# Later weight stores, a regrouped output layer and a store on two queues, in a fused attention and two-layer kernel

## The chip, the cores and the metric

The kernel runs on one core of a Trainium2 chip. The metric is the device time of one execution in microseconds (us). Three timed executions of the kernel before took 1245.21, 1245.39 and 1239.18 us, so the median is 1245.21. The trace that is read below belongs to another execution of the same kernel, which took 1240.78 us.

## The reference

All inputs are float32 (the weights arrive as 64-bit values and are narrowed on the chip). Cut to what is computed:

```python
def sm_attn(qq, kk, vv):                      # softmax(scale * qq kk^T) vv, per batch and head
    s = scale * (qq @ kk.T);  s = s - s.max(-1)
    a = exp(s);  return (a / (a.sum(-1) + 1e-9)) @ vv
p_packed = sm_attn(p, k, v)                   # 8 batches, 8 heads, 32 packed rows, 64 columns
x = sm_attn(q, p_packed, p_packed)            # 576 rows per batch and head -> x: 4608 x 512
x = max(x @ w1, x @ w2, x @ w3) @ moe_w_out   # 512 -> 768 -> 512
h = x @ w_in                                  # 512 -> 2048
g = max(h, 0) + log1p(exp(-abs(h)))           # softplus
out = g @ w_out                               # 2048 -> 512
```

## The kernel before

The first 507 us of the span hold the attention and the maxout layer, batch by batch. The change touches only what follows: the last two products, called layer 3 (`h = x @ w_in` and the softplus) and layer 4 (`g @ w_out`).

Both work on the transposed activations, in five blocks of tokens (index `c`): three blocks of 2 x 512 columns and two of 2 x 384. Both use a fast matrix scheme with seven products in place of eight (`PRODUCTS`). Each product keeps float32 accuracy by splitting each operand into a high and a low part and adding three matmuls: high by high, high by low, low by high.

A block's layer 3 has eight rounds (`j`, 42 matmuls each). Its layer 4 has 28 steps (`v`, 12 matmuls each). A step of layer 4 needs the high part `ghi` (made by ScalarE, line 126) and the low part `glo` (made by VectorE, line 128) of a slice of `g`. Both are made three steps ahead: `split_g(c, v + 3)` stands behind `layer4(c, v)`. There are three buffers each, so ScalarE can make the part of step v + 3 only once TensorE has done step v. Inside a step (lines 1125 to 1142) stand two row groups `i`, two accumulators `b` (PSUM banks) and three matmuls each. The weight tile holds high parts (`wl` = 0) and low parts (`wl` = 1).

Weights come in 16 tiles per block, eight for layer 3 and eight for layer 4. In the first block (c = 0) they are made on the way. SyncE loads raw tile s (`wu`, 896 KB from `wof` for layer 4). ScalarE and VectorE split it in two parts (`split_weights`, part 0 and part 1). The finished tile `wc` (1792 KB) stays in a ring of three for use, and is also stored to memory (`wic`, `woc`; line 1017) for the later blocks, which only load it again (`get_weights`, line 1025). The raw tiles share two buffers with the raw activations `xu` of the next block (`load_x2`, line 923), so a raw tile can be loaded only after the split of an older one has freed its buffer.

The order of the work is written out by hand: each engine gets its instructions in the order in which the program issues them (a manual schedule), and executes them in that order. In the first block `jobs[v]` lists what is issued behind step v: splits, loads, sums and splits of the next block's activations. In layer 3 the lists `aside[0]` to `aside[3]` stand between the products. SyncE issues nearly all transfers, one after another; an instruction that waits there holds back those behind it.

`done[v]` lists the results: `result` (VectorE adds and transposes) and `store` (line 1162, four transfers or more on the queues that it is given). In the last block the results of the second token half leave behind steps 19 and 27, those of the first half behind step 23.

Of the kernel before, what the change touches and what calls it, by code (L numbers as in the profile page):

```python
# [8 lines left out]
F32 = mybir.dt.float32  # L9
# [10 lines left out]
def packed_attention_maxout_softplus(  # L20
# [22 lines left out]
    nc = tc.nc  # L43
# [31 lines left out]
    FP = F2 // 2  # L75
    wi32 = dram.tile([FP, P, 4, 2, P], F32, name="wi32")
    wic = dram.tile([FP, P, 2 * 7 * 2 * P], F32, name="wic")
    wof = dram.tile([len(PRODUCTS), FP, P, 2 * P], F32, name="wof")
    woc = dram.tile([FP, P, 2 * 7 * 2 * P], F32, name="woc")
# [41 lines left out]
    def split(src, hi, lo, engine=nc.vector):  # L121
        for _ in split_steps(src, hi, lo, engine):
            pass
# [717 lines left out]
    for n in range(1, B):  # L841
        for slot in range(F1 + KC):
# [22 lines left out]
            if n + 1 == B:  # L865

                if slot == 0:
# [12 lines left out]
                    pairs, wus, xus, x2 = {}, {}, {}, {}  # L880
# [24 lines left out]
                    def pair_tile(s):  # L905
                        t = ring[s % 3].tile([P, 2, 7, 2, P], F32R, tag="ring", name="wc")
                        pairs[s] = t
                        return t
# [100 lines left out]
    def split_weights(s, part):  # L1009
        if part == 0:  # L1010
            pair_tile(s)
        a, b = ((0, 4), (4, 7))[part]
        u, t = wus[s], pairs[s]
        split(u[:, a + 1 : b + 1], t[:, 0, a:b], t[:, 1, a:b])
        if part == 1:
            wus.pop(s)
            nc.sync.dma_start(
                out=(wic[s] if s < FP else woc[s - FP]),
                in_=t.rearrange("p h a k x -> p (h a k x)").bitcast(F32),
            )  # L1020

    def get_weights(s):
        if STEP <= s < STEP * NCH:
            r = s % STEP
            nc.sync.dma_start(
                out=pair_tile(s).rearrange("p h a k x -> p (h a k x)").bitcast(F32),
                in_=(wic[r] if r < FP else woc[r - FP]),
            )

    def bank(name):  # L1030
        return psp.tile([P, CH], F32, tag="ps", name=name)
# [53 lines left out]
    def form(c, name, u, n, engine):  # L1085


        us = slice(u, u + n)
        a11, a12, a21, a22 = (
            g[i, k][:, us, : BLOCKS[c][1]] for i in range(2) for k in range(2)  # L1090
        )
        s2 = None if name == "S3" else row(c, 1 + u // 2)
        out, in0, in1, op = {
            "S3": (a21, a11, a21, ALU.subtract),
            "S2": (s2, a22, a21, ALU.subtract),
            "S1": (a11, a11, s2, ALU.add),
            "S4": (a12, a12, s2, ALU.subtract),
        }[name]
        engine.tensor_tensor(out=out, in0=in0, in1=in1, op=op)  # L1099
# [16 lines left out]
    def layer4(c, v):  # L1116

        pos, name, wide = v // NU, PRODUCTS[v // NU], BLOCKS[c][1]
        ghi, glo = gt.pop(v)
        first = name in ("P1", "P5", "P2")  # L1120
        if first and v % NU == 0:
            acc[CHAIN[name]] = [bank("ps_4") for b in range(2)]
        ps = acc[CHAIN[name]]
        todo = []
        for i in range(2):
            u = 2 * (v % NU) + i
            tile_no, at = divmod(pos * FP + u, 7)
            w = pairs[STEP * c + FP + tile_no]
            for wl, x in ((0, ghi), (1, ghi), (0, glo)):
                for b in range(2):  # L1130
                    todo.append((b, u, w[:, wl, at, b], x[:, i], wl == 0 and x is ghi, x is glo))
        if v == NV - 1:
            todo.sort(key=lambda m: m[0])
        for b, u, l, r, head, tail in todo:
            nc.tensor.matmul(  # L1135
                ps[b][:, :wide],
                l,
                r,
                start=first and u == 0 and head,
                stop=u == FP - 1 and tail,  # L1140
                skip_group_check=not first,
            )
# [50 lines left out]
    with tc.manual_schedule(engines={E.PE, E.DVE, E.Activation, E.Pool, E.SP}):  # L1193
        for c in range(NCH):
            more, last = parts[c + 1], c == NCH - 1
            for j in range(FP):
                aside = {0: [], 1: [], 2: [], 3: []}
                if c == 0:
                    if j + 2 < FP:
                        aside[0].append((sum_pair, j + 2, nc.gpsimd))  # L1200
                    for part in range(2):
                        aside[1 + part].append((split_weights, j + 2, part))
                    aside[3].append((load_weights, j + 4))
                    if j and j % 2 == 0:
                        aside[1].append((form, c, "S3", j - 2, 2, nc.vector))
                elif more:
                    for part in range(2):
                        if j == 1 + part:
                            aside[0].append((load_x2, c + 1, part))
                        if j == 3 + part:  # L1210
                            aside[1].append((sum_x2, c + 1, part, nc.gpsimd))
                if j == FP - 1:
                    for v in range(2):
                        aside[2].append((split_g, c, v))
                layer3(c, j, aside)
                if c:
                    form(c, "S3", j, 1, nc.gpsimd)
                get_weights(STEP * c + j + 3)
            mid[c] = cp.tile([P, 10 * CH], F32, tag="h", name="mid")
            split_g(c, 2)  # L1220
            jobs = {v: [] for v in range(-1, NV)}
            if c == 0:
                jobs[0].append((form, c, "S3", FP - 2, 2, nc.vector))
                for t in range(6):
                    v = 7 * t // 2 + 1
                    for part in range(2):
                        jobs[v + part].append((split_weights, FP + t + 2, part))
                    if t >= 1 and FP + t + 3 < STEP:
                        jobs[v + 1].append((load_weights, FP + t + 3))
                jobs[2].append((load_x2, c + 1, 0))  # L1230
                for part, v in enumerate((7, 12, 16, 21)):
                    jobs[v - 1].append((sum_x2, c + 1, part))
                    jobs[v].append((split_x2, c + 1, part))
                    if part + 1 < more:
                        jobs[v].append((load_x2, c + 1, part + 1))
            else:
                for part, v in zip(range(more), (12, 14, 18, 22)):
                    if part > 1:
                        jobs[v - 1].append((sum_x2, c + 1, part))
                    jobs[v].append((split_x2, c + 1, part))  # L1240
                    if part + 2 < more:
                        jobs[v].append((load_x2, c + 1, part + 2))
            for i in range(NU):
                for name, v in (("S2", 0), ("S1", 4), ("S4", 8)):
                    jobs[v + i].append((form, c, name, 2 * i, 2, nc.vector))
            done = {
                3: [(keep_sum, c, "X", 0)],
                11: [(keep_sum, c, "X", 1)],
                13: [(out_tile, c, 0), (result, c, 0, 0, "Z", 0)],
                15: [(keep_sum, c, "Y", 2)],  # L1250
                19: [(out_tile, c, 1), (result, c, 1, 1, "X", 2)],
                23: [(result, c, 0, 1, "Y", 1), (store, c, 0, (0, 1), [nc.sync])],
                27: [(result, c, 1, 0, "X")],
            }
            if last:
                done[19].append((store, c, 1, (1,), [nc.sync]))
                done[27].append((store, c, 1, (0,), [nc.sync, nc.scalar]))
            else:
                done[27].append((store, c, 1, (0, 1), [nc.sync]))
            for v in range(NV):  # L1260
                layer4(c, v)
                if v + 3 < NV:
                    split_g(c, v + 3)
                for fn, *args in done.get(v, []) + jobs[v]:
                    fn(*args)
                for t in range(FP):
                    if (7 * t + 6) // 2 == v:
                        pairs.pop(STEP * c + FP + t)
                        get_weights(STEP * c + FP + t + 3)
# [36 lines left out]
```

## Time and profile before

| what | value |
| --- | --- |
| three timed runs | 1245.21, 1245.39, 1239.18 us (median 1245.21) |
| profiled execution | 1240.78 us, of which the span of its instructions is 1239.0 us |
| TensorE busy | 1207.5 us (97% of the span) |
| VectorE, ScalarE, GpSimd busy | 831.5, 526.8, 213.2 us |
| chain of work that ended last | TensorE 87%, DMA 5%, VectorE 4% of the span |
| mean granted TensorE clock | 0.991 of full speed |

"Busy" of TensorE is rough: matmuls overlap and their ends are modelled, so the time from one matmul's start to the next is the better measure. PEld is TensorE's weight load, which runs beside the matmuls. PE, DVE, ACT, POOL and SP are TensorE, VectorE, ScalarE, GpSimd and SyncE; a "q" behind the name stands for the engine's sequencer (issues and waits).

### The profile page before, as it was taken

The page shows a single profiled execution, that of the slowest core. Times are in us where ns is not written, and L with a number is a line of the kernel's source. Part 1 is how long each engine was busy: PE and PEld are TensorE (multiplying, and loading weights), DVE is VectorE, ACT ScalarE, POOL GpSimd, SP SyncE. Part 2 cuts the span into 40 slices and gives each one's busy share as a digit, 9 for nine tenths or more (in the row PEclk, how much of TensorE's full clock was granted, in tenths as well). Part 3 has the DMA queues.
Part 4 walks back from the last instruction along what each step waited for, and adds up shares of the span by engine and source line. Part 5 has one row for each costly group of instructions (what it writes and reads, how often), then busy time and mean ns, then how long its engine had stood idle before and what let it go on. Part 6 is the DMA issues. An engine that isn't in the chain of part 4 may idle for free.

```text
span 1239.0 us, 21402 instructions
## 1 busy us (share of the span) xinstructions
PE 1207.5 (97%) x8599; PEld 1062.0 (86%) x8599; DVE 831.5 (67%) x1182; ACT 526.8 (43%) x782; POOL 213.2 (17%) x224
## 2 busy tenths in 40 slices
PE   8899999999999999999977999999999999999998
PEld 6788989898989899888755788888888899999998
DVE  2975747565757659677977456894568845885584
ACT  4744343434343435445544224452244523452342
POOL 1422212223333322230000031000310003000100
PEclk9999999999999999999988999999999999999999
DMA  9978485869695731768655965469544597768764
GB/s 235 284 214 220 136 226 164 217 188 249 169 269 173 201 99 57 283 248 305 212 195 204 312 227 178 178 212 307 211 178 179 195 337 273 259 224 326 250 255 140
DMA packets 117283, 272.26 MB, mean 220 GB/s; under 512 B 14784, under 2 KB 90304, under 8 KB 106944
## 3 DMA queue, kind: packets, MB, share of 16 engines
q1 hardware_dynamic: 111776, 261.26, 66.8%
q10 hardware_dynamic: 5408, 9.64, 2.2%
q8 instruction: 67, 1.10, 0.4%
q14 instruction: 32, 0.26, 0.1%
HBM read 211.09 MB, written 59.77 MB: 219 GB/s over the span
## 4 chain that ended last, share of the span: by engine, by line
PE 87%; DMA 5%; DVE 4%; issue 2%; ACT 1%; SPq 1%; DVEq 0%; ACTq 0%
PE ps L482 31%; PE ps L1042 27%; PE ps L1135 24%; PE ps_w L460 2%; DMA wu<-wof 2%; PE ps_s L287 1%; DVE glo L128 1%; DMA wc<-wic 1%; DMA wraw<-in_moe_w_dram 1%; PE ps_v L358 1%; PE ps_e L331 1%; DMA xu<-x2d 1%; DVE wc L128 0%; DVE x2lo L128 0%; DMA praw<-in_p_dram 0%
## 5 line engine op out<-in xcount | busy, mean ns | idle before, releaser
L1042 PE MATMUL ps<-x2hi,wc 128*128 128x512 f32 (+1 forms) x1120 | 322.2, 367 | 0.5 <-DMA wc<-wic 0.5
L1135 PE MATMUL ps<-ghi,wc 128*128 128x512 f32 (+1 forms) x1120 | 287.7, 378 | 9.1 <-ACT ghi L126 9.0
L1056 DVE TENSOR_TENSOR h<-h,ps 128x512 f32<-128x512 f32 (+1 forms) x280 | 173.6, 633 | 155.5 <-PE ps L1042 116.1
L1135 PEld LDWEIGHTS ps<-ghi,wc 128*128 128x128 f32 x1120 | 209.5, 191 | 42.1 <-ACT ghi L126 10.8
L1042 PEld LDWEIGHTS ps<-x2hi,wc 128*128 128x128 f32 x1120 | 207.0, 188 | 27.8 <-issue 1.5
L1042 PE MATMUL ps<-x2lo,wc 128*128 128x512 f32 (+1 forms) x560 | 205.6, 367 | 0.0
L1077 ACT ACTIVATE a<-h 128x512 f32<-128x512 f32 (+1 forms) x160 | 89.2, 584 | 220.2 <-DVE h L1056 211.6
L1135 PE MATMUL ps<-glo,wc 128*128 128x512 f32 (+1 forms) x560 | 168.3, 379 | 8.0 <-DVE glo L128 7.9
L128 DVE TENSOR_TENSOR glo<-a,ghi 128x1024 fp32r<-128x1024 f32 (+1 forms) x120 | 132.0, 1110 | 33.8 <-ACT ghi L126 33.2
L126 ACT ACTIVATE ghi<-a 128x1024 fp32r<-128x1024 f32 (+1 forms) x120 | 114.6, 971 | 92.7 <-PE ps L1135 88.7
L1099 POOL TENSOR_TENSOR a<-a,a 128x512 f32<-128x512 f32 (+1 forms) x32 | 36.8, 1151 | 567.3 <-ACT a L1077 567.3
L1135 PEld LDWEIGHTS ps<-glo,wc 128*128 128x128 f32 x560 | 104.4, 190 | 27.5 <-DVE glo L128 12.7
L482 PE MATMUL ps<-a2hi,pwhi 128*128 128x288 f32 x576 | 127.6, 303 | 0.1
L482 PE MATMUL ps<-a2hi,pwlo 128*128 128x288 f32 x576 | 123.3, 296 | 0.4 <-DVE pwlo L128 0.4
L482 PE MATMUL ps<-a2lo,pwhi 128*128 128x288 f32 x576 | 123.1, 295 | 0.0
L1042 PEld LDWEIGHTS ps<-x2lo,wc 128*128 128x128 f32 x560 | 105.1, 188 | 13.0
L511 DVE TENSOR_TENSOR m<-ps,m 128x576 f32<-128x576 f32 x96 | 72.4, 754 | 49.3 <-PE ps L482 47.3
L482 PEld LDWEIGHTS ps<-a2hi,pwhi 128*128 128x128 f32 x576 | 91.7, 189 | 15.0 <-ACT m L509 5.3
L128 POOL TENSOR_TENSOR hlo<-m,hhi 128x576 fp32r<-128x576 f32 x41 | 59.2, 1443 | 238.2 <-ACT hhi L126 221.7
L128 DVE TENSOR_TENSOR pwlo<-ps_w,pwhi 128x1024 fp32r<-128x1024 f32 (+1 forms) x40 | 44.5, 1113 | 78.6 <-ACT pwhi L126 78.5
L482 PEld LDWEIGHTS ps<-a2hi,pwlo 128*128 128x128 f32 x576 | 92.6, 188 | 0.7 <-DVE pwlo L128 0.7
L482 PEld LDWEIGHTS ps<-a2lo,pwhi 128*128 128x128 f32 x576 | 92.5, 188 | 0.3 <-DVE a2lo L128 0.3
(107 smaller groups left out, 1522.3 us busy)
## 6 DMA issues: line engine op xcount, KB each, us to landing
wc<-wic SPq DMA_DIRECT2D x32, 1792.0 KB
wc<-woc SPq DMA_DIRECT2D x32, 1792.0 KB
qraw<-in_q_dram SPq DMA_DIRECT2D x112, 140.0 KB
wic<-wc SPq DMA_DIRECT2D x8, 1792.0 KB
woc<-wc SPq DMA_DIRECT2D x8, 1792.0 KB
kraw<-in_k_dram SPq DMA_DIRECT2D x96, 140.0 KB
vt<-in_v_dram SPq DMA_DIRECT2D x8, 1152.0 KB
wraw<-in_moe_w_dram SPq DMA_DIRECT2D x18, 512.0 KB
```

What stands on the lines that cost most here:

```text
L126: nc.scalar.activation(out=hi, in_=src, func=AF.Copy)
L128: engine.tensor_tensor(out=lo, in0=src, in1=hi.bitcast(F32), op=ALU.subtract)
L287: nc.tensor.matmul(ps[G][cols, hh, :HS], w[rows, cols], x[rows, g, hh * HS : hh * HS + HS], start=True, stop=True,)
L331: nc.tensor.transpose(ps[: 32 * TI, i // hi, (i % hi) * P : (i % hi) * P + P], e[:, i], ident,)
L460: nc.tensor.matmul(ps[cols, G, : units * P].rearrange("p (w x) -> p w x", w=units), ppT[n][rows, cols], wsb[rows, 4 * c : 4 * c + units, g ...
L482: nc.tensor.matmul(o, w, xx, start=first, stop=last)
L511: nc.vector.tensor_tensor(out=m, in0=ps[:, :, :HS], in1=ms[n, f], op=ALU.max)
L1042: nc.tensor.matmul(out, l, r, start=(i == 0), stop=(i == len(terms) - 1))
L1056: add(out=h[:, o], in0=h[:, a], in1=ps, op=ALU.add)
L1077: nc.scalar.activation(out=g[half, k][:, j, :wide], in_=h[:, 2 * k + half], func=AF.Softplus)
L1099: engine.tensor_tensor(out=out, in0=in0, in1=in1, op=op)
L1135: nc.tensor.matmul(ps[b][:, :wide], l, r, start=first and u == 0 and head, stop=u == FP - 1 and tail, skip_group_check=not first,)
```

## The change

Three edits:

1. The store of a finished weight tile is a function of its own (`put_weights`). It is issued behind the next load in layer 3, and one step after the split in layer 4. The first load of the next block's activations moves to stand before a store.
2. A step of layer 4 goes through the accumulators outside and the three matmuls inside, and these stand in the order high by high, high weights by low activations, low weights by high activations.
3. In the last block, the store of the first half's results behind step 23 uses SyncE's and ScalarE's queues in turn.

```diff
@@ split_weights, put_weights
         if part == 1:
             wus.pop(s)
-            nc.sync.dma_start(
-                out=(wic[s] if s < FP else woc[s - FP]),
-                in_=t.rearrange("p h a k x -> p (h a k x)").bitcast(F32),
-            )
+
+    def put_weights(s):
+        nc.sync.dma_start(
+            out=(wic[s] if s < FP else woc[s - FP]),
+            in_=pairs[s].rearrange("p h a k x -> p (h a k x)").bitcast(F32),
+        )
@@ layer4
-            for wl, x in ((0, ghi), (1, ghi), (0, glo)):
-                for b in range(2):
-                    todo.append((b, u, w[:, wl, at, b], x[:, i], wl == 0 and x is ghi, x is glo))
+            for b in range(2):
+                for wl, x in ((0, ghi), (0, glo), (1, ghi)):
+                    todo.append((b, u, w[:, wl, at, b], x[:, i], wl == 0 and x is ghi, wl == 1))
@@ layer 3, first block
-                    aside[3].append((load_weights, j + 4))
+                    aside[3] += [(load_weights, j + 4), (put_weights, j + 2)]
@@ layer 4, first block
                     if t >= 1 and FP + t + 3 < STEP:
                         jobs[v + 1].append((load_weights, FP + t + 3))
-                jobs[2].append((load_x2, c + 1, 0))
+                    if t == 0:
+                        jobs[v + 1].append((load_x2, c + 1, 0))
+                    jobs[v + 2].append((put_weights, FP + t + 2))
@@ results
-                23: [(result, c, 0, 1, "Y", 1), (store, c, 0, (0, 1), [nc.sync])],
+                23: [
+                    (result, c, 0, 1, "Y", 1),
+                    (store, c, 0, (0, 1), [nc.sync, nc.scalar] if last else [nc.sync]),
+                ],
```

SyncE, first block, layer 4, before. `woc<-wc` is the store of a finished tile, `wu<-wof` the load of a raw weight tile, `xu<-x2d` the load of activations.

```order
L923 DMA xu_7472<-x2d_61 128x2x128 x4
L1017 DMA woc_65<-wc_7515 128x3584
L998 DMA wu_7538<-wof_64 128x7x256
L923 DMA xu_7584<-x2d_61 128x2x128 x4
L1017 DMA woc_65<-wc_7606 128x3584
L998 DMA wu_7629<-wof_64 128x7x256
```

The same place now:

```order
L923 DMA xu_7471<-x2d_61 128x2x128 x4
L1019 DMA woc_65<-wc_7449 128x3584
L998 DMA wu_7537<-wof_64 128x7x256
L1019 DMA woc_65<-wc_7515 128x3584
L923 DMA xu_7584<-x2d_61 128x2x128 x4
L998 DMA wu_7628<-wof_64 128x7x256
L1019 DMA woc_65<-wc_7606 128x3584
```

Each load of a raw tile stood directly behind the store of the tile whose split frees its buffer; now that store stands behind the load. An activation load stands between a store and the second of the loads.

TensorE, the first step of layer 4 in the last block, before (`ps_11806` and `ps_11807` are the two accumulators):

```order
L1135 MATMUL ps_11806<-ghi,wc 128x384
L1135 MATMUL ps_11807<-ghi,wc 128x384
L1135 MATMUL ps_11806<-ghi,wc 128x384
L1135 MATMUL ps_11807<-ghi,wc 128x384
L1135 MATMUL ps_11806<-glo,wc 128x384
L1135 MATMUL ps_11807<-glo,wc 128x384
```

The same place now:

```order
L1137 MATMUL ps_11806<-ghi,wc 128x384
L1137 MATMUL ps_11806<-glo,wc 128x384
L1137 MATMUL ps_11806<-ghi,wc 128x384
L1137 MATMUL ps_11807<-ghi,wc 128x384
L1137 MATMUL ps_11807<-glo,wc 128x384
L1137 MATMUL ps_11807<-ghi,wc 128x384
```

The matmul with the low part `glo` moved from fifth place to second; it uses the same weights as the one ahead of it.

ScalarE at the end of the program, before (`ghi` of the last four steps, then the last store):

```order
L126 ACTIVATE ghi_12202<-a11_11333 128x2x384
L126 ACTIVATE ghi_12218<-a11_11333 128x2x384
L126 ACTIVATE ghi_12234<-a11_11333 128x2x384
L126 ACTIVATE ghi_12262<-a11_11333 128x2x384
L1162 DMA out_0_dram<-o_12165 32x12x64 x2
```

The same place now:

```order
L126 ACTIVATE ghi_12202<-a11_11333 128x2x384
L126 ACTIVATE ghi_12218<-a11_11333 128x2x384
L126 ACTIVATE ghi_12234<-a11_11333 128x2x384
L1164 DMA out_0_dram<-o_12058 32x6x128 x4
L126 ACTIVATE ghi_12262<-a11_11333 128x2x384
L1164 DMA out_0_dram<-o_12165 32x12x64 x2
```

Four transfers, of which the first waits for VectorE's result, now stand ahead of the high part for the last step.

## Rows read from the trace of the kernel before

**Rows 1.** Busy time by stretch (columns: us, engines, TensorE clock, DMA share, GB/s).

```profile
582.80:687.20 104.40, 87.30 (x337) 65.67 (x336) 82.17 (x92) 48.27 (x55) 0.00 (x0) 0.92 0.63 211
764.30:842.90 78.60, 78.60 (x337) 63.20 (x336) 66.17 (x71) 38.68 (x43) 1.29 (x1) 1.00 0.56 190
```

**Rows 2.** Waits, 582.8 to 687.2 us (total, times, longest, in us).

```profile
ACT wc L126 <- DMA wu<-wof: 30.0, 4, 10.0
DVE wc L128 <- ACT wc L126: 17.8, 4, 7.6
```

**Rows 3.** Timeline of SyncE's queue (start us, us, what).

```profile
623.06 0.33 SPq L1017 DMA_DIRECT2D woc<-wc  x1
623.43 0.43 SPq L998 DMA_DIRECT2D wu<-wof  x1
```

**Rows 4.** Timeline of ScalarE (in brackets idle time before, and its releaser).

```profile
632.54 1.06 ACT L126 ACTIVATE wc<-wu 128x1024 fp32r<-128x1024 f32 x1 [9.37 <-DMA wu<-wof]
```

**Rows 5.** Busy time by stretch, one store and load, and VectorE's full stretch.

```profile
588.20:617.40 29.20, 27.33 (x115) 20.92 (x113) 29.11 (x29) 15.45 (x17) 0.00 (x0) 1.00 0.65 216
...
623.00:628.50 5.50, 5.43 (x23) 4.06 (x22) 4.57 (x5) 0.17 (x1) 0.00 (x0) 1.00 0.96 334
628.50:632.60 4.10, 1.81 (x8) 1.13 (x6) 0.00 (x0) 0.06 (x1) 0.00 (x0) 0.99 0.65 224
```

**Rows 6.** Timeline of VectorE, splits of weight tiles in layer 4 of the first block.

```profile
622.08 0.95 DVE L128 TENSOR_TENSOR wc<-wu,wc 128x768 fp32r<-128x768 f32 x1
...
633.63 1.22 DVE L128 TENSOR_TENSOR wc<-wu,wc 128x1024 fp32r<-128x1024 f32 x1 [6.06 <-ACT wc L126]
...
638.51 0.95 DVE L128 TENSOR_TENSOR wc<-wu,wc 128x768 fp32r<-128x768 f32 x1
...
650.35 1.23 DVE L128 TENSOR_TENSOR wc<-wu,wc 128x1024 fp32r<-128x1024 f32 x1 [2.85 <-ACT wc L126]
...
654.10 0.95 DVE L128 TENSOR_TENSOR wc<-wu,wc 128x768 fp32r<-128x768 f32 x1
...
666.94 1.23 DVE L128 TENSOR_TENSOR wc<-wu,wc 128x1024 fp32r<-128x1024 f32 x1 [7.62 <-ACT wc L126]
```

**Rows 7.** Timeline of TensorE, behind the second of these waits.

```profile
634.59 2.07 PE L1135 MATMUL ps<-ghi,wc 128*128 128x512 f32 x4 [4.29 <-ACT ghi L126]
```

**Rows 8.** The chain that ended last, in order of time (start us, us, what).

```profile
140.75 20.98 PE ps L482 x156
...
843.18 76.16 PE ps L1042 x336
919.34 78.71 PE ps L1135 x336
998.06 58.27 PE ps L1042 x336
1056.32 59.36 PE ps L1135 x336
```

**Rows 9.** Timeline of TensorE, the last step of the last block.

```profile
1231.55 0.52 PE L1135 MATMUL ps<-ghi,wc 128*128 128x384 f32 x2
...
1232.08 0.52 PE L1135 MATMUL ps<-ghi,wc 128*128 128x384 f32 x2
```

**Rows 10.** Timeline of VectorE and TensorE, third step of the fourth block's layer 4.

```profile
1059.83 1.83 DVE L128 TENSOR_TENSOR glo<-a,ghi 128x768 fp32r<-128x768 f32 x2 [1.74 <-ACT ghi L126]
...
1060.40 0.87 PE L1135 MATMUL ps<-ghi,wc 128*128 128x384 f32 x4
```

**Rows 11.** Timeline of the end: ScalarE, SyncE's queue, VectorE, ScalarE's queue.

```profile
1227.16 0.85 ACT L126 ACTIVATE ghi<-a 128x768 fp32r<-128x768 f32 x1 [1.27 <-PE ps L1135]
...
1228.93 0.92 DVE L128 TENSOR_TENSOR glo<-a,ghi 128x768 fp32r<-128x768 f32 x1
...
1229.04 6.28 SPq L1162 DMA_DIRECT2D out_dram<-o  x10
...
1234.49 0.91 ACTq L1162 DMA_DIRECT2D out_dram<-o  x2
```

**Rows 12.** Line 1135: its engine sat idle before it until (us, times).

```profile
  DVE glo L128: 20.6, 17
```

## The prediction

> **What bounds the kernel now.** I read the chain of waits first: TensorE holds 87% of it, so only what makes TensorE wait, or its own pace, can move the end. Then the busy times by stretch. Layer 4 of the first block takes 104.4 us, the same 336 matmuls in the second block 78.6 us [rows 1]. Some 26 us are lost in this one stretch, at a mean clock of 0.92. The waits inside it say to whom: four times ScalarE waited for a load of raw weights, 30.0 us in all, and VectorE in turn 17.8 us for ScalarE's copies [rows 2]. ScalarE executes in order, so while it waits it makes no `ghi` for TensorE.
>
> One such load shows why it is late. SyncE issues the store of a tile at 623.06 and the load at 623.43 [rows 3]; ScalarE can read the raw tile at 632.54 [rows 4], 9.1 us after the issue. From 623.0 to 628.5 us 334 GB/s were moved, 1.84 MB, which is the 1792 KB of the store; from 628.5 to 632.6 it was 224 GB/s, 0.92 MB, which is the 896 KB of the load [rows 5]. The load's bytes come behind the store's, 5 us late.
>
> Everywhere behind this stretch TensorE is the bound, and there only its pace counts. Layer 3 and layer 4 have 336 matmuls each per block. At 512 columns they take 76.16 and 78.71 us, at 384 columns 58.27 and 59.36 us [rows 8].
>
> **Part 1, stores behind loads.** Four times VectorE waits for the copy of a raw tile (`FP+4` to `FP+7`). The last three waits are 6.06, 2.85 and 7.62 us [rows 6]; the four are 17.8 [rows 2], so the first is 1.3. The load is issued when VectorE has finished the second part of an earlier tile, and is due when VectorE comes to the first part of the next. What VectorE does between is cover: from 622.08 + 0.95 to 633.63 - 6.06 it is 4.5 us, for the next 8.0, for the last 4.3 [rows 6]. The first had more than 9 us of it, as its wait shows. Against the cover stand 0.4 us until SyncE issues [rows 3, 6], the load itself, and the copy of 1.06 us [rows 4].
>
> How long a load takes without a store ahead of it no row shows. The lower bound is 4.1 us, the stretch in which it had the queue to itself [rows 5], without a start; the upper bound is 9.1, if the order changes nothing. I take 4.5, near the lower end, because the two stretches show its bytes cleanly behind the store's. The need is then 0.4 + 4.5 + 1.1 = 6.0 us. Left are waits of 1.5 and 1.7 us at the tiles with 4.5 and 4.3 us of cover, none at the others: 3.2 us of the 17.8. The gain is 14.6; with 4.1 us it is 15.4, with 9.1 us about 3. The Trainium skill (DMA: Bandwidth & Descriptors, "Anatomy of one DMA") fits 2.0 us plus bytes by 436 GB/s to a DMA issued another way; an estimate by it is 4.1 us here, which would make the gain 15.4.
>
> More can't be had, since VectorE becomes the bound: from 588.2 to 617.4 us it is busy 29.11 of 29.20 us [rows 5], with no wait for a load. Its 82.2 us of work [rows 1] and the waits left fill the shorter stretch. TensorE's lost time at the lower clock comes back within this gain and not beside it: four matmuls took 2.07 us behind a wait of 4.29 us [rows 7], when VectorE had nothing to do either. If one of the waits that are left still brings the clock to its lower level, up to 4 us of the gain are lost.
>
> The stores moved away run beside splits that need no transfer, and go ahead of activations that are due four steps later (11 us). The ring gives a tile's slot back only ten steps on. In layer 3 of the first block TensorE has no wait to lose, so I count nothing.
>
> **Part 2, order of the matmuls.** Same instructions, same count; the pace can change. Per matmul layer 3 takes 226.7 ns at 512 columns and 173.4 at 384, layer 4 takes 234.3 and 176.7 [rows 8]. Operand shapes and weight tiles are alike. Layer 3 uses a weight operand for two matmuls in succession, then one once; layer 4 never uses one twice running. Changing the accumulator is not it: the last step, which does one accumulator after the other, still takes 0.53 us for three matmuls [rows 9], 177 ns each. And the attention's products, which also change the accumulator each time but keep weights over four and two matmuls, take 20.98 us for 156 of 288 columns [rows 8], 134.5 ns. Above the time of the columns at 2.4 GHz (120, 160, 213 ns) that is 14 ns, in layer 3 13 ns at both widths, in layer 4 17 and 21. The new order is layer 3's, so I take layer 3's pace: 2.55 us in each of two blocks and 1.09 in each of two, 7.3 us. In the first block VectorE is the bound and the faster pace gives nothing. The bounds are 0 (the order is not the cause) and 7.3.
>
> The Trainium skill speaks against this part (TensorE: Matmul & The Clock Gate, "Back-to-back issue gap"): a single matmul's gap is the columns by 2.4 GHz plus 2.5 ns, whatever the weights. By it nothing would be gained. The rows agree with it nowhere, since both layers are slower and differ; but it keeps the case alive in which the cause lies elsewhere.
>
> It also has a price. `glo` is needed after one matmul and no longer after four, 3 x 234 ns = 0.7 us sooner. In the later blocks it is close in the third step: TensorE starts it at 1060.40, and VectorE makes two low parts in 1.83 us from 1059.83 [rows 10], so the first is there at about 1060.8, needed at 1060.6. With the quicker pace I count 0.3 us in each block of 384 and nothing in the wide ones, 0.6 us. In the first block VectorE is not held back by it; but TensorE's last step ends 0.7 us later behind VectorE.
>
> **Part 3, two queues.** ScalarE's four transfers stand ahead of the last `ghi`. They can go when VectorE's result is there, which is when SyncE's first is issued, 1229.04. An issue on ScalarE takes 0.46 us (two in 0.91), so it is free at 1230.9, with 0.85 us for `ghi` and about 0.95 for `glo` at 1232.7 [rows 11]. Before, `ghi` was made at 1227.16 [rows 11]. The last step starts at 1231.55 [rows 9] and needs `glo` one matmul later, 1231.7: 1.0 us late, with the quicker pace 1.2. Nothing comes back: SyncE's ten issues from 1229.04 end at 1235.3, the last two being those of the last result, which ScalarE issues at 1234.49 as before.
>
> **Sum.** -14.6 + 0.7 - 7.3 + 0.6 + 1.2 = -19.4 us against the profiled execution's 1240.8 (1.8 of it outside the span): 1221.4. The median shown, 1245.2, is 4.4 us higher, the fastest run 1.6 lower. For a median I add some of that: 1223.
>
> **Rivals.**
> - *The order of matmuls gains nothing.* 1240.8 - 14.6 + 0.7 + 0.3 + 1.0 = 1228.2; at the median's footing 1232.
> - *The loads stay slow*, because stores issued a moment later share the same 16 engines with them. For it: the DMA share was 0.96 beside the store [rows 5]. Against it: the store now follows the load by an issue. The gain is 3 in place of 14.6: about 1233, without the matmul gain 1240.
> - *Slower: the earlier `glo`.* TensorE waited 17 times for it in layer 4 [rows 12]. If each wait grows by 0.7 us and is passed on (TensorE's delay holds the buffer for ScalarE's next high part, that one VectorE's), this costs 11.9 us and, with the tail's 1.2 and no gain elsewhere, gives 1254. It decides from where VectorE has no other work to fill the time; against it, VectorE ran without a gap over 29 us while TensorE waited [rows 5].
>
> **How the numbers follow.** Forecast 0.55, the order gaining nothing 0.25, slow loads 0.14, slower 0.06. The forecast alone spans 1215 to 1227: loads at 4.1 us and the fastest run's footing below, a spell at the lower clock above. The range goes on to the second case: 1213 to 1235. A measurement here can tell about 0.5% (6 us) from no change. Below 1239 lie the first two cases and most of the third: faster 0.89; within 0.5% 0.07; slower 0.04.
>
> **What would show it.** Right: first-block layer 4 near 90 us, ScalarE's waits for `wu<-wof` at a few us in place of 30, VectorE almost without idle time there; later layer 4 at 76.2 and 58.3 us; before the last step a wait of TensorE of about 1 us, behind ScalarE's issues. Wrong: loads that still take 9 us; layer 4 still at 78.7 and 59.4 us; waits for `glo` in the later blocks above 1 us each; no wait at the end.

## The result, and the profile after

| | time in us |
| --- | --- |
| kernel before | 1243.28, median of 5 (1239.18 to 1245.39) |
| changed kernel | 1233.44, median of 5 (1230.52 to 1234.49) |
| ratio | 0.9919, 95% interval 0.9894 to 0.9944 |
| profiled execution, before and after | 1240.78 and 1230.52 |

The kernel is faster by about 10 us. The forecast was 1223, some 20 us faster; 1233.44 lies inside the range, near its slow end, and 1.4 us above what the forecast's first rival gives (1232). Lines of the code that stood at 1042, 1135 and 1162 stand at 1044, 1137 and 1164 in the changed kernel.

The view to read first is the same as before, busy time by stretch. This is layer 4 of the first block and of the second, for the two rows in [rows 1].

```profile
583.20:675.60 92.40, 84.06 (x338) 64.60 (x337) 82.22 (x93) 48.81 (x55) 0.00 (x0) 0.96 0.70 243
752.10:830.80 78.70, 78.70 (x338) 63.18 (x337) 66.12 (x70) 38.79 (x43) 1.30 (x1) 1.00 0.54 188
```

The first block's layer 4 has lost 12 us, from 104.4 to 92.4, with VectorE's work unchanged at 82.2 us. The second block's has lost nothing. The waits of the first block's layer 4 say the same [rows 2]:

```profile
ACT wc L126 <- DMA wu<-wof: 6.7, 2, 5.7
...
DVE wc L128 <- ACT wc L126: 5.1, 2, 3.0
...
ACT wc L126 <- DMA xu<-x2d: 3.6, 1, 3.6
```

ScalarE's waits for raw weights fell from 30.0 to 10.3 us, VectorE's for ScalarE's copies from 17.8 to 5.1. The 10.3 are the 6.7 of the first line and the 3.6 of the last: the profile names the activation load there, but the instruction that waits splits a raw weight tile and reads no activations. One load shows why the waits are shorter. First SyncE's queue, then ScalarE's and VectorE's timelines [rows 3, 4, 6]:

```profile
622.30 0.36 SPq L998 DMA_DIRECT2D wu<-wof  x1
622.70 0.56 SPq L1019 DMA_DIRECT2D woc<-wc  x1
```

```profile
628.71 1.06 ACT L126 ACTIVATE wc<-wu 128x1024 fp32r<-128x1024 f32 x1 [5.75 <-DMA wu<-wof]
```

```profile
629.80 1.23 DVE L128 TENSOR_TENSOR wc<-wu,wc 128x1024 fp32r<-128x1024 f32 x1 [2.99 <-ACT wc L126]
...
654.65 1.22 DVE L128 TENSOR_TENSOR wc<-wu,wc 128x1024 fp32r<-128x1024 f32 x1 [2.09 <-ACT wc L126]
```

The load now stands ahead of the store, and ScalarE reads its tile 6.4 us after the issue in place of 9.1. The chain of waits gives the pace behind the first block, for the rows in [rows 8]:

```profile
752.14 78.77 PE ps L1137 x336
830.91 76.17 PE ps L1044 x336
907.08 78.78 PE ps L1137 x336
985.86 58.27 PE ps L1044 x336
```

Layer 4 still takes 78.8 us where layer 3 takes 76.2. The new order of the matmuls did nothing to it. At the end of the kernel, ScalarE's and TensorE's timelines before the last step [rows 9, 11]:

```profile
1217.37 2.26 ACTq L1164 DMA_DIRECT2D out_dram<-o  x4
1219.74 0.84 ACT L126 ACTIVATE ghi<-a 128x768 fp32r<-128x768 f32 x1 [5.52 <-DMA out_dram<-o]
```

```profile
1219.24 0.34 PE L1137 MATMUL ps<-ghi,wc 128*128 128x384 f32 x1
1220.63 0.44 PE L1137 MATMUL ps<-ghi,wc 128*128 128x384 f32 x1 [1.06 <-ACT ghi L126]
1221.63 0.44 PE L1137 MATMUL ps<-glo,wc 128*128 128x384 f32 x1 [0.56 <-DVE glo L128]
```

ScalarE issues four transfers and only then makes the last `ghi`. From the first of these matmuls to the second are 1.39 us, and 1.00 from there to the third, where matmuls stand 0.17 apart: 2.0 us are lost.

Where the 10 us come from, stage by stage (from a stage's first matmul to the next stage's; the last layer 4 to its own last matmul): first block's layer 4 -12.3, the layer 3 behind it -0.7, the two layers 4 at 512 columns +0.1, the fourth block's layer 4 -0.2, the fifth's layer 3 +0.9 (a wait for a weight tile), its layer 4 +1.5. The sum is -10.7. What lies ahead of layer 3 took 0.6 us longer and varies by up to 7 us from run to run; therefore the table below also gives the time from layer 3's first matmul to the end of the span.

### The profile page after: what moved, and what is told of

Same layout as the page of the kernel before. It is cut to its first block, busy times and chain, and to the rows that moved or that the text cites. A ratio compares the mean times of both kernels' runs of the same rounds, so it can differ in the third digit from the quotient of the medians.

```text
span 1228.7 us, 21279 instructions
## 1 busy us (share of the span) xinstructions
PE 1204.3 (98%) x8599; PEld 1059.8 (86%) x8599; DVE 832.9 (68%) x1182; ACT 527.5 (43%) x782; POOL 217.7 (18%) x224
## 4 chain that ended last, share of the span: by engine, by line
PE 86%; DVE 8%; DMA 3%; issue 1%; ACT 1%; SPq 0%; DVEq 0%; ACTq 0%
PE ps L482 31%; PE ps L1044 27%; PE ps L1137 22%; PE ps_w L460 2%; DVE glo L128 2%; PE ps_s L287 1%; DVE x2lo L128 1%; DVE wc L128 1%; PE ps_v L358 1%; DMA wc<-wic 1%; PE ps_e L331 1%; PE ps_k L232 1%; DMA qraw<-in_q_dram 1%; DMA xu<-x2d 1%; DVE a L1101 1%
## 5 line engine op out<-in xcount | busy, mean ns | idle before, releaser
L1137 PE MATMUL ps<-ghi,wc 128*128 128x512 f32 (+1 forms) x1120 | 329.1, 374 | 1.6 <-ACT ghi L126 1.6
L1058 DVE TENSOR_TENSOR h<-h,ps 128x512 f32<-128x512 f32 (+1 forms) x280 | 173.3, 633 | 154.8 <-PE ps L1044 118.1
L1137 PE MATMUL ps<-glo,wc 128*128 128x512 f32 (+1 forms) x560 | 211.5, 378 | 8.6 <-DVE glo L128 8.5
L1044 PEld LDWEIGHTS ps<-x2lo,wc 128*128 128x128 f32 x560 | 105.1, 188 | 13.2
L128 POOL TENSOR_TENSOR hlo<-m,hhi 128x576 fp32r<-128x576 f32 x41 | 59.2, 1444 | 238.7 <-ACT hhi L126 227.9
```

The source lines that it names most:

```text
L128: engine.tensor_tensor(out=lo, in0=src, in1=hi.bitcast(F32), op=ALU.subtract)
L1044: nc.tensor.matmul(out, l, r, start=(i == 0), stop=(i == len(terms) - 1))
L1058: add(out=h[:, o], in0=h[:, a], in1=ps, op=ALU.add)
L1137: nc.tensor.matmul(ps[b][:, :wide], l, r, start=first and u == 0 and head, stop=u == FP - 1 and tail, skip_group_check=not first,)
```

## The experiments

Two questions were open: which edit brought the gain, and why layer 4 kept its own pace. "L4" is layer 4, timed as above; it and the time from layer 3 to the end come from one profiled execution of each kernel. Each ratio is to runs of the kernel before that were timed beside it (medians 1243.14 to 1245.52 us); the first row shows one such set.

| kernel | median us (range, runs) | ratio to before (95%) | layer 3 to end | first L4 | L4 at 512 | L4 at 384 |
| --- | --- | --- | --- | --- | --- | --- |
| before | 1243.15 (1239.84–1248.52, 23) | | 732.4 | 104.6 | 78.7, 78.7 | 59.4, 59.2 |
| changed kernel | 1233.44 (1230.52–1234.49, 5) | 0.9919 (0.9894–0.9944) | 721.5 | 92.3 | 78.8, 78.8 | 59.1, 60.7 |
| e1_stores | 1230.24 (1228.44–1232.09, 5) | 0.9896 (0.9872–0.9920) | 719.5 | 91.5 | 78.7, 78.7 | 59.4, 59.2 |
| e2_order | 1242.51 (1241.12–1246.78, 12) | 0.9997 (0.9982–1.0012) | 732.2 | 105.9 | 78.8, 78.8 | 59.1, 58.5 |
| e3_queue | 1244.83 (1240.74–1248.24, 12) | 1.0010 (0.9994–1.0027) | 734.5 | 105.1 | 78.7, 78.7 | 59.4, 60.7 |
| e4_no_queue | 1232.37 (1227.47–1235.72, 6) | 0.9908 (0.9880–0.9936) | 719.3 | 92.5 | 78.8, 78.8 | 59.1, 58.5 |
| p4_act_store | 1229.08 (1228.21–1234.15, 5) | 0.9880 (0.9856–0.9904) | 718.5 | 91.2 | 78.8, 78.8 | 59.5, 58.5 |
| s1_place | 1235.54 (1233.97–1237.90, 6) | 0.9919 (0.9895–0.9943) | 725.9 | 104.7 | 76.2, 76.2 | 58.2, 58.1 |
| b1_best | 1226.91 (1224.03–1234.16, 6) | 0.9873 (0.9839–0.9907) | 715.1 | 92.4 | 76.4, 76.5 | 59.1, 58.5 |
| b2_best | 1223.32 (1221.91–1226.91, 5) | 0.9836 (0.9814–0.9858) | 712.8 | 91.4 | 76.2, 76.2 | 58.2, 58.1 |

### One edit at a time

Each of the three edits was put alone into the kernel before; the fourth kernel has edits 1 and 2.

```diff
  e1_stores (and e4_no_queue, with the new order)
-            nc.sync.dma_start(out=(wic[s] ...          # in split_weights
+    def put_weights(s): ...                            # issued behind the next load
  e2_order
-            for wl, x in ((0, ghi), (1, ghi), (0, glo)):
-                for b in range(2):
+            for b in range(2):
+                for wl, x in ((0, ghi), (0, glo), (1, ghi)):
  e3_queue
-                (store, c, 0, (0, 1), [nc.sync])
+                (store, c, 0, (0, 1), [nc.sync, nc.scalar] if last else [nc.sync])
```

> The kernel before with the first edit alone (later stores of weight tiles, later load order). If the trace of the changed kernel is read rightly, layer 4 of the first block takes about 92 us in place of 104.6, the later blocks' layer 4 stay at 78.7 and 59.4 us, and the time falls by 12 us (ratio near 0.990). If part of the first block's gain came from the other matmul order, the stretch stays above 95 us.

> The kernel before with the matmul order of layer 4 alone. Theory of the prediction (repeating a weight operand sets the pace): later blocks at 76.2 us (512 columns) and 58.3 us (384), 7 us less. Reading of the changed kernel's trace: no gain at 512 columns (78.7 us), about 1 us less per block at 384 behind a first wait, first block's layer 4 unchanged near 104 or 1 us longer for the earlier low part: between 1 us faster and 1 us slower in all.

> The kernel before with the two-queue store alone. Prediction: TensorE waits 1.0 to 1.2 us before the last step. The changed kernel's trace shows 2.0 us there, since ScalarE's four issues took 2.26 us beside SyncE's; in this order, where the low part is the fifth matmul, 0.5 us less: 1 to 2 us slower, ratio 1.001. Rival: the stores leave earlier and the end comes 1 us sooner.

> The changed kernel without the two-queue store. If that edit costs what the trace shows, this one is 2 us faster than the changed kernel: a ratio near 0.990 to before, no wait of TensorE before the last step. If the store on two queues gains something that the trace hides, it is as slow as the changed kernel or slower.

From layer 3 to the end the edits change the time by -12.9, -0.2 and +2.1 us alone, -11.0 together, and the changed kernel has -10.9. That it agrees so closely is in part luck, since stages that an edit doesn't touch differ by some tenths of a us from run to run (0.8 of the +2.1). Edit 1 is the whole gain. This is its first layer 4, for the row in [rows 1]:

```profile
586.80:678.70 91.90, 83.50 (x339) 63.70 (x338) 82.16 (x92) 48.47 (x55) 0.00 (x0) 0.98 0.69 244
```

Edit 2 is worth nothing at 512 columns and 0.9 us at 384. It lengthens the first block's layer 4 by 1.0 to 1.3 us, most of which the layer 3 behind it gives back. Edit 3 costs 1.5 us in the one stage that it touches, the last layer 4, and 2.1 there in the changed kernel (60.7 us against 58.5 in e4_no_queue). The whole times of e2_order and e3_queue can't be told from the kernel before, nor e4_no_queue's from the changed kernel's; the stages tell them apart. In the kernel with edit 3 alone the last step waits as in the changed one:

```profile
1235.16 0.62 PE L1135 MATMUL ps<-ghi,wc 128*128 128x384 f32 x2 [0.60 <-ACT ghi L126]
1236.15 0.44 PE L1135 MATMUL ps<-glo,wc 128*128 128x384 f32 x1 [0.38 <-DVE glo L128]
```

### Is it any order of the matmuls?

Three kernels like e4_no_queue tried other orders: six matmuls in a row into one accumulator, as layer 3 has them; no weight operand twice running in layer 4; and the same in layer 3, which should lose its pace if the repeats give it.

```diff
  p1_six
-        if v == NV - 1:
+        if True:                      # todo.sort(key=lambda m: m[0]) in every step
  p2_noshare
-                for wl, x in ((0, ghi), (0, glo), (1, ghi)):
+                for wl, x in ((0, glo), (1, ghi), (0, ghi)):
  p3_l3 (layer 3)
-            for a, b in ((0, 0), (0, 1), (1, 0))
+            for a, b in ((0, 0), (1, 0), (0, 1))
```

> The changed kernel without the two-queue store, and each step of layer 4 does all six matmuls of one accumulator, then six of the other (three and three in the changed kernel, as layer 3's six). Theory R, a repeated weight operand sets the pace: later blocks as before this edit, 78.7 us at 512 columns, 58.3 us plus waits at 384. Theory B, the run of matmuls into one accumulator sets it: six are needed at 512 columns, which then take 76.2 us. Theory M, something in layer 4 other than the order (its operands' place): 78.7 us at 512.

> The changed kernel without the two-queue store, with the three matmuls of an accumulator in the order high weights by low activations, low weights by high activations, high by high: three in a row into one accumulator, no weight operand twice running. Theory R: at 384 columns the pace is 176.7 ns, as in the kernel before (59.4 us a block). Theory B: 173.3 ns (58.3 us plus waits), as in the changed kernel. Theory S, a wait in mid-stream sets off the quicker pace whatever the order: 173.3 ns as well, from the first wait on. The low part is needed one matmul sooner, 0.2 us more per wait.

> The changed kernel without the two-queue store, with layer 3's three matmuls in the order high by high, low weights by high activations, high weights by low activations: no weight operand twice running, still six into one accumulator. Theory R: layer 3 goes from 76.2 to 78.7 us at 512 columns and from 58.3 to 59.4 at 384. Theories B and M: layer 3 stays at 76.2 and 58.3.

A timed run of each gave 1230.22, 1229.27 and 1231.06 us. One run says little of the whole time, so here and below, where there is only one, the stages are read. Layer 4 at 512 columns stayed at 78.8, 78.9 and 78.8 us, and layer 3 kept 76.2 and 58.3 us without any repeat. Neither the repeated operand nor the run into one accumulator sets the pace.

### Where the stores go

```diff
-                    jobs[v + 2].append((put_weights, FP + t + 2))
+                    jobs[v + 4].append((put_weights, FP + t + 2, nc.scalar))
```

> The changed kernel without the two-queue store, and layer 4's eight weight stores of the first block go by ScalarE's queue, four steps behind the first part of the split, where ScalarE has already read the next raw tile. If the load is late because the store issued 0.4 us behind it shares the engines, a load alone takes 4.5 us in place of 5.3 to 6.4 and the first block's layer 4 shrinks from 92.3 to some 89 us. If the load is slow by itself, it stays within 1 us of 92.3. The issues on ScalarE cost 0.4 us each.

Here no store is near the load, which can be read on SyncE's queue and ScalarE's timeline:

```profile
653.88 0.36 SPq L998 DMA_DIRECT2D wu<-wof  x1
```

```profile
659.03 1.06 ACT L126 ACTIVATE wc<-wu 128x1024 fp32r<-128x1024 f32 x1 [3.72 <-DMA wu<-wof]
```

It takes 5.15 us, with activation loads issued 2 us behind it; another one, with nothing near it, takes 5.35. In the changed kernel two loads with the store right behind them took 6.4 and 6.5. So both expectations hold in part: the load is slower by itself than the 4.5 us taken, and the store behind it adds about 1.2. The stores on ScalarE's queue shorten the stage by 1.4 us against e4_no_queue (91.2 to 92.5); the whole time differs by less than the intervals show.

### Where the operand lies

What was left is the operand itself. The program's layout puts layer 3's operand (`x2hi`, `x2lo`) and all weight tiles at byte 2016 of a stretch of 2048 in each partition, and `ghi` and `glo` at byte 1664. Asking for the other side of the memory moved them by only 352 bytes, to 2016. A second kernel gave the first 12 steps of layer 4 layer 3's operand; a third began a new sum with every three matmuls. (The second leaves out layer 4's own operand in those steps, the third the sums over the units.)

```diff
  t1_right
-    gp = ctx.enter_context(tc.tile_pool(name="gp", bufs=3, reuse_waits="tile"))
+    gp = ctx.enter_context(tc.tile_pool(name="gp", bufs=3, side="right", reuse_waits="tile"))
  t2_x2
+                    r = x2[c][x is glo][:, min(u, 6), i, :wide] if c and v < 12 else x[:, i]
  t3_start
-                start=first and u == 0 and head,
-                stop=u == FP - 1 and tail,
+                start=head,
+                stop=tail,
```

> As e4_no_queue, but the buffers of ghi and glo lie at the other end of the memory, where layer 3's operand and the weight tiles lie. Theory P (layer 4's pace at 512 columns comes from where the moving operand lies): 226.7 ns per matmul in layer 4 of the second and third block, 76.2 us each in place of 78.8; the time some 5 us below 1232. Rival A (it comes from something else in the step): 234.3 ns and 78.8 us, as in every run so far; 1228 to 1234 us.

> As e4_no_queue, but in the first 12 of the 28 steps of layer 4, behind the first block, the matmuls take layer 3's operand (x2hi, x2lo) in place of ghi and glo, so part of what is computed is another thing. Theory P, and every theory that blames the moving operand (its place, or that it was just written): 226.7 ns per matmul in the first 12 steps at 512 columns and 234.3 in the other 16. Rival A (weights, banks, accumulation or the other engines' work): 234.3 in all 28 steps.

> As e4_no_queue, but every three matmuls of layer 4 into one accumulator begin a new sum, as every six do in layer 3; sums over the units are left out. Theory C (matmuls that add to a bank that was last written long before run slower): 226.7 ns at 512 columns in layer 4. Rival A or P: 234.3 ns. At 384 columns 173.4 behind the first waits in either case.

A timed run of each gave 1227.13, 1228.55 and 1234.29 us. The chain of waits of t1_right:

```profile
755.88 76.45 PE ps L1137 x336
832.33 76.16 PE ps L1044 x336
908.49 76.47 PE ps L1137 x336
```

And of t2_x2:

```profile
754.93 77.61 PE ps L1138 x336
832.54 76.17 PE ps L1044 x336
908.71 77.61 PE ps L1138 x336
```

352 bytes take 2.3 us off each layer 4 at 512 columns. With layer 3's operand the pace is 226.7 ns in exactly the first 12 steps and 234.3 in the other 16; the new sums leave it at 234.2. So the cause is the place. Two more kernels tried six places (one for each step modulo 3, by spacers of 32 to 352 bytes), and one kept `ghi` and `glo` but moved one of the three buffers of weight tiles from 2016 to 1664.

```diff
  o1_place: pads (32, 96, 224); o2_place: pads (128, 320, 352)
+    for n, pad in enumerate(pads):
+        if pad > at:
+            spacer = ctx.enter_context(tc.tile_pool(name=f"pad{n}", bufs=1)) ...
+        gps.append(ctx.enter_context(tc.tile_pool(name=f"gp{n}", bufs=1, reuse_waits="tile")))
  r1_ring
+                        if name == "ring2":
+                            spacer.tile([P, 88], F32, name="pad")       # 352 bytes
```

> As e4_no_queue, but the three pairs of ghi and glo buffers (step modulo 3) begin 32, 96 and 224 bytes further on, so at byte 1696, 1760 and 1888 of a stretch of 2048. Theory M (the remainder by 64 bytes decides, 32 as with layer 3's operand): all three 226.7 ns at 512 columns. Theory M128: 234, 227, 227. Theory M256: 234, 227, 234. Theory S (only the same place as the weight tiles, 2016, is fast): 234 in all three.

> As o1_place, with 128, 320 and 352 bytes: byte 1792, 1984 and 2016. The third is the place that was fast, in the same kernel: 226.7 ns. By M, M128, M256 and S the first two run at 234 ns; if 1984 is fast as well, closeness to the weight tiles' place counts and not a remainder.

> As e4_no_queue, with ghi and glo at their old place (1664), but one of the three buffers of weight tiles (ring2) moved by 352 bytes to 1664. Theory R (the two places must agree): in the second and third block layer 4 runs at 226.7 ns while its weights come from ring2 (a third of it) and at 234.3 otherwise, and layer 3 at 234.3 ns with ring2 and 226.7 otherwise. Theory Q (the moving operand's place alone): layer 3 stays at 226.7 everywhere, layer 4 at 234.3.

A timed run of each gave 1231.48, 1227.34 and 1229.87 us. Mean time from one matmul's start to the next at 512 columns, worked out from the starts inside a step or round, for o1_place and o2_place from the fourth matmul of a step on:

```
operand at, weights at   distance   ns per matmul
2016, 2016                   0      226.7
1984, 2016                  32      233.1
1888, 2016                 128      233.2
1792, 2016                 224      233.3
1760, 2016                 256      227.0
1696, 2016                 320      233.3
1664, 2016                 352      234.3
2016, 1664 (layer 3)       352      233.4
1664, 1664                   0      226.7
```

Only the distances 0 and 256 are fast, as "M256" expected: what counts is what is left of the distance when whole stretches of 256 bytes are taken off (modulo 256). The 128 x 128 pieces of a weight tile begin 512 bytes apart, so each row stands for distances 512, 1024 and 1536 larger as well; the 256 itself rests on one place in one run. Two steps of o1_place, first the end of one at 1760, then one at 1888:

```profile
784.32 0.62 PE L1143 MATMUL ps<-ghi,wc 128*128 128x512 f32 x2
...
785.00 0.62 PE L1143 MATMUL ps<-ghi,wc 128*128 128x512 f32 x2
...
785.68 0.62 PE L1143 MATMUL ps<-ghi,wc 128*128 128x512 f32 x2
...
787.07 0.63 PE L1143 MATMUL ps<-ghi,wc 128*128 128x512 f32 x2
...
787.76 0.63 PE L1143 MATMUL ps<-ghi,wc 128*128 128x512 f32 x2
...
788.47 0.62 PE L1143 MATMUL ps<-ghi,wc 128*128 128x512 f32 x2
```

The `ghi` pairs of the first are 0.68 us apart, which is three matmuls, those of the second 0.69 and 0.71. And r1_ring shows that it is a distance and not a place: layer 4 becomes fast at the old place when the weights come from the moved buffer, and layer 3 slow. TensorE's timeline in its layer 3, where the second round's weights, the first from the moved buffer, begin at 685.8:

```profile
683.57 0.61 PE L1049 MATMUL ps<-x2hi,wc 128*128 128x512 f32 x2
684.02 0.39 PE L1049 MATMUL ps<-x2lo,wc 128*128 128x512 f32 x1
684.25 0.61 PE L1049 MATMUL ps<-x2hi,wc 128*128 128x512 f32 x2
684.70 0.39 PE L1049 MATMUL ps<-x2lo,wc 128*128 128x512 f32 x1
684.93 0.61 PE L1049 MATMUL ps<-x2hi,wc 128*128 128x512 f32 x2
685.38 0.39 PE L1049 MATMUL ps<-x2lo,wc 128*128 128x512 f32 x1
685.61 0.63 PE L1049 MATMUL ps<-x2hi,wc 128*128 128x512 f32 x2
686.08 0.40 PE L1049 MATMUL ps<-x2lo,wc 128*128 128x512 f32 x1
686.31 0.62 PE L1049 MATMUL ps<-x2hi,wc 128*128 128x512 f32 x2
686.78 0.40 PE L1049 MATMUL ps<-x2lo,wc 128*128 128x512 f32 x1
687.01 0.62 PE L1049 MATMUL ps<-x2hi,wc 128*128 128x512 f32 x2
```

The starts of the `x2hi` pairs are 0.68 us apart (three matmuls) up to 685.61 and 0.70 behind it.

### The place alone, and the best version

s1_place is the kernel before with the place changed as in t1_right. b1_best is p4_act_store with it, and b2_best is b1_best with the old order of the matmuls.

```diff
  s1_place, b1_best, b2_best
+    gp = ... side="right" ...
  b2_best against b1_best
-            for b in range(2):
-                for wl, x in ((0, ghi), (0, glo), (1, ghi)):
+            for wl, x in ((0, ghi), (1, ghi), (0, glo)):
+                for b in range(2):
```

> The kernel before with ghi and glo 352 bytes further on and nothing else changed: order, stores and tail as before. Theory R (both operands begin at the same byte, counted in stretches of 256): layer 4 takes layer 3's pace, 226.7 ns in the second and third block (76.2 to 76.5 us each in place of 78.7) and 173.4 ns in the two blocks of 384 (58.3 to 58.9 in place of 59.3); 4.5 to 7 us in all, a ratio to the kernel before of about 0.995. If the old order matters as well, as the prediction had it: 78.7 and 59.3 us stay, ratio 1.000.

> p4_act_store (edits 1 and 2, layer 4's weight stores on ScalarE's queue, no second queue at the tail) with ghi and glo at byte 2016. By theory P 4.7 us below p4_act_store (two blocks of 512 columns by 2.33 us): about 1225, ratio to the kernel before 0.985. By rival A, in which t1_right was one good run, 1229 to 1230.

> b1_best with the old order of the matmuls: edit 1, layer 4's weight stores on ScalarE's queue, ghi and glo 352 bytes further on; no new order, no second queue at the tail. If the order costs waits for glo and gives nothing: 76.16 and 58.25 us in the later layers 4, some 1.8 us less than b1_best from the start of layer 3 to the end (715.1 us there), about 1223 to 1226, ratio 0.984. If the new order is worth something once the place is right: no better than b1_best.

The chain of waits of s1_place, with the old order:

```profile
765.40 76.16 PE ps L1135 x336
841.56 76.16 PE ps L1042 x336
917.72 76.16 PE ps L1135 x336
993.88 58.27 PE ps L1042 x336
...
1169.39 58.26 PE ps L1135 x336
```

That is layer 3's pace to 0.03 us, and 2.55 us less in each wide block and 1.1 less in each narrow one: 7.3 us, the whole term that the prediction gave to the order. (From layer 3 to the end it is 6.5 us, since the first layer 4 and two layers 3 took 0.9 longer in this run. The medians' interval, 0.57 to 1.05% or 7 to 13 us, holds the 7.3 near its lower end.)

b2_best is the fastest kernel here, 20 us below the one before. The old order is the better one: the chain of waits shows its layer 4 without a wait,

```profile
753.56 76.16 PE ps L1137 x336
829.72 76.16 PE ps L1044 x336
905.88 76.16 PE ps L1137 x336
982.04 58.48 PE ps L1044 x336
1040.52 58.24 PE ps L1137 x336
```

while b1_best spends 0.3 us more in each wide layer 4 and 0.9 and 0.5 in the narrow ones, 1.9 in all. The two ratios' intervals overlap; the stages of the traces separate them. Against p4_act_store, b1_best's wide layers 4 gain the 4.7 us that were expected; from layer 3 to the end it is 3.4, since its first layer 4 took 1.2 us longer.

## Why the prediction went wrong, point by point

- **Where the time was lost** was right: VectorE's work set the first layer 4, late loads stretched it, and the clock came back inside that gain. The granted clock of the stretch rose from 0.92 to 0.96. The condition that the prediction attached to this did come about: behind a wait of TensorE of 3.6 us its granted clock was still 0.50, the lower of its two levels (1.2 GHz), from 634.0 to 640.8 us. In the kernel before it was 0.50 for 10.2 and 6.8 us. The "up to 4 us" set beside it was not worked out, and no run separates what the stretch cost.
- **Part 1, stores behind loads**: right, and mis-sized by 1 to 2 us. Expected was 14.6 less 0.7 for the earlier `glo`; the changed kernel shows 12.3, and edit 1 alone 13.0. In the first block's layer 3 the later stores changed nothing, as counted (76.20 us before and after). The term that was too small is the load: I took 4.5 us near the lower end, and it takes 5.2 to 5.4 without a store near it and 6.4 to 6.5 with one right behind it. VectorE's waits came to 5.1 us in place of 3.2. The page's fit that was named beside it (the Trainium skill, DMA: Bandwidth & Descriptors, "Anatomy of one DMA") made an estimate of 4.1 us for it, though it is fitted to DMAs issued another way; the loads without a store near them took over 1 us longer.
- **Part 2, order of the matmuls**: this is the step that failed. "The new order is layer 3's, so I take layer 3's pace" gave 7.3 us; e2_order measured 0.06 us the wrong way in each wide block, and 0.2 and 0.7 us less in the narrow ones, which come from something else (next point). The rows showed two layers with two paces, I found one difference between them and took it for the cause. "Operand shapes and weight tiles are alike" was true, and silent on where the operands lie, which is what differed. The size of the term was exact: s1_place has all 7.3 us, with the old order.
- **The price of part 2**: right in kind. I had 0.6 us for waits in the narrow blocks and nothing in the wide ones; with the place right they cost 1.4 and 0.6. In the changed kernel they were covered, because at 384 columns a wait switched the pace from 176.7 to 173.3 ns (below), which gave back 0.2 and 0.7 us.
- **Part 3, two queues**: right in mechanism, 2.0 us in place of 1.2. Four issues on ScalarE took 2.26 us, 0.57 each, where I counted 0.46 from two [rows 11]; and the first matmul of the last step, not just the second, waited.
- **The sum**: -12.3 and +2.0, with -0.9 at 384 columns, +0.9 for a weight tile in the fifth block that I had not looked at, and the other small items above. The rival "the order of matmuls gains nothing" (1228 for the profiled execution, which took 1230.5; 1232 for a median) had a chance of 0.25 and is what happened. That its time came out within 2 us is in part luck: it had 1.6 us too much for the loads and 1.0 too little for the queues, and neither the gain at 384 columns nor the one in the second block's layer 3. The rival of loads that stay slow fell: the store behind a load costs it about 1 us, not the 4 that the one ahead of it did. The slower one, through the earlier `glo`, fell too: TensorE waited oftener for `glo` in layer 4, but the total rose only from 20.6 [rows 12] to 23.0 us, as line 1137's row on it says. (Both rows count a wait at the weight load and often again at the matmul behind it: the 17 before are 11 and 6, all in the first block. So that rival's price, 17 times 0.7 us, was at most 11 times 0.7, or 7.7.)

```profile
  DVE glo L128: 23.0, 26
```

## What to carry to other kernels

When two loops of the same matmuls run at different paces, compare everything about their operands, the addresses too, before taking a visible difference in order for the cause; a kernel that gives one loop the other's operand separates them in one run. Let the moving operand and the weights begin at the same byte, counted in stretches of 256, where the weights are loaded for every matmul, as here; other types and shapes were not measured. And a load that somebody waits for goes ahead of a store that nobody waits for, while transfers issued by an engine that still has work for the last step belong on another queue.

## What the hardware showed beyond that

- With a weight load per matmul (128 x 128, fp32r), 512 columns take 226.7 to 227.0 ns when the operands' places agree modulo 256 bytes and 233.1 to 234.3 when they do not; 384 columns take 173.3 and up to 176.7. The Trainium skill (SBUF — State Buffer, "Who interferes with whom") says that TensorE reads the moving operand and the weights through two independent ports; by that their places should not matter to each other, and here they do, by 3%. That the two reads meet in the memory would explain it, but no run shows the mechanism.
- At 384 columns with disagreeing places both paces occur, in p2_noshare within one block and with the same instructions. In the kernel before it is 176.7 ns throughout; in e2_order a wait in the first steps of a block is followed by 173.3 for nearly all of the rest, and in p2_noshare a later wait led back. At 512 columns no wait did that. Why is open.
- The same eight stores take longer to issue, from the third of each queue on, when two queues issue them at once. In the changed kernel's tail the four issues on ScalarE took 0.39, 0.45, 0.53 and 0.77 us while SyncE issued its own four, which took 0.32, 0.44, 0.55 and 0.79. In the kernel before, eight on SyncE alone took 0.32 to 0.46 each; e3_queue and e4_no_queue repeat the two cases. Why is not shown: the larger stores of the first block's results took 0.35 to 1.25 us on SyncE alone.
